# A decode kernel's last microseconds: the last head as single-column products for both chunks, the projections as one row, the output as four rows

## The chip, the cores and the metric

The kernel runs on one core of one Trainium2 chip. The metric is the device time of one execution in microseconds (us), lower is better. The profile was taken in one execution of each kernel; its span is 1.7 to 1.9 us shorter than the time of the same execution, so spans are compared with spans and times with times.

## The reference, cut to what matters

```python
# H, Sk, Dh = 32, 65536, 128;  D = 512;  F = 1792;  one token
g = sigmoid((x * gate_w).sum(-1))
q = (x @ wq).reshape(H, Dh)
p = softmax(q @ k_cache.T * Dh**-0.5)        # per head, over 65536 keys
a = concat(p @ v_cache) @ wo                 # 4096 -> 512
b = (silu(x @ w_gate) * (x @ w_up)) @ w_down
out = g * a + (1 - g) * b                    # 512 numbers
```

The two caches are 1.07 GB in bf16, and each byte is used once.

## The kernel before

The caches stream through three slots of 8 MB. A head is two chunks of 32768 keys, a partition holding 256 of them (`KPP`), so there are 64 chunks of keys and 64 of values; the last head is chunks 62 and 63. For a chunk, VectorE multiplies keys by the query, TensorE adds the products up by identity matmuls (`block`), VectorE sums the eight columns left over (`gather`), ScalarE takes the exponential. The values are then weighted in one of two forms. The wide form, used for chunks 0 to 62, has 64 matmuls with 4 columns of probabilities as weights and 512 columns of values moving; the wanted result is the diagonal, picked by four small products:

```python
def pv(n):
    ...
    mms(..., O_ps,
        [(P_sb[n % 2][:, g : g + VB], v[:, g : g + VB, :].rearrange("p a b -> p (a b)"))
         for g in range(0, KPP, VB)], ...)
    if c == last:
        act("O_sb", O_sb, O_ps, ACT.Copy, ["O_ps"], ["O_sb"])
        pending.append(h)          # diagonal() comes later
```

The column form has one matmul for each of the 256 keys of a partition, with a 128x128 tile of values as weights and one column moving. Before, it was used for chunk 63 only, piece by piece as the values land:

```python
V_END = [KPP // 2, KPP // 4, KPP // 8, KPP // 16, KPP // 16]      # 128, 64, 32, 16, 16
...
load("k", n, [EK] * (KPP // EK)); load("v", n, V_END)
turn_outputs(1)
rows("b_ps", wd, ..., hT, ...)                 # 4 x 14 one-column products into m_x
diagonal()
for i, j in enumerate(range(0, KPP, EK)):      # four blocks of the last keys
    block(n, j, EK)
    if i == 0:
        ...                                    # rest = (1 - g) * b
        rows("a_ps", wo, ..., M, ...)          # 4 x 32 one-column products
    if i == 2:
        ...                                    # rest += g * a   [128, 4]
    ...
for m in V_END:
    mms(("c", at), m_c[:, 0:1],
        [(v[:, j, :], P_sb[n % 2][:, j : j + 1]) for j in range(at, at + m)], ...)
    if at == 0:
        norm(h, H)
    at += m
dve("o_last", ... m_c[:, 0:1] * tot ...)                       # [128, 1]
rows("l_ps", wo_last, ..., o_last, "o_last", [0])              # 4 one-column products
dve("out_sb", ... m_x[:, :OT] * gval + rest ...)               # [128, 4]
dma("out", out[0, 0].rearrange("(p b) -> p b", b=OT), out_sb, ...)   # 128 pieces of 8 B
```

In chunk 62 the normalizer of the 31 heads before (`norm`: one matmul, a sum, a reciprocal; then `outputs`) is emitted right after the last block's sums, ahead of the gathers of the last two blocks; `turn_outputs(0)` follows behind them.

The softmax here doesn't subtract the row's maximum and nothing guards it: scores larger than these inputs give would overflow.

## Time and profile before

| | before |
|---|---|
| time, median of the 3 runs before the prediction | 2521.22 us (2519.79 to 2521.41) |
| span of the profiled execution | 2519.9 us |
| mean rate of the transfers over the span | 432 GB/s |
| last values landed | 2511.90 us |
| last column product ended | 2514.67 us |
| output issued / landed | 2515.62 / 2518.59 us |

The landings in this document are the completions that the trace records for each transfer; all times are counted from the start of the span.

From the page of the kernel before: the span, the transfers' busy share in 40 equal slices in tenths, and the bytes read with their rate.

```profile
span 2519.9 us, 15461 instructions
...
DMA  9999999999999999999999999999999999999998
...
HBM read 1087.77 MB, written 0.00 MB: 432 GB/s over the span
...
```

The stream of the caches is the kernel. In 39 of 40 slices the transfer engines are 90% busy or more.

The next lines are stretches of one microsecond at the end (start:end, length, then busy time and count of TensorE, weight loads, VectorE, ScalarE and GpSimd, then TensorE's granted clock as a share of full speed, the transfer engines' share and the rate in GB/s).

```profile
...
2510.00:2511.00 1.00, 1.00 (x44) 1.00 (x42) 0.29 (x2) 0.00 (x0) 0.00 (x0) 0.62 0.37 143
2511.00:2512.00 1.00, 0.44 (x17) 0.38 (x15) 0.00 (x0) 0.00 (x0) 0.00 (x0) 0.50 0.08 33
...
```

The stream runs dry between 2511 and 2512 us. What comes after is not covered by it.

From the timeline of the kernel before (start, duration, engine, line, operation, output and inputs, shapes, count; in brackets the idle time before and what ended it):

```profile
...
2463.50 0.42 DVE L478 TENSOR_REDUCE tot<-m_x 128x31 f32<-128x248 f32 x1 [4.14 <-PE m_x L251]
...
2464.51 0.68 DVE L363 TENSOR_REDUCE S_sb_81<-S_ps_101 128x64 f32<-128x512 f32 x1
...
2466.23 15.46 PE L251 MATMUL O_ps<-slot_65,P_sb_83 128*4 128x512 bf16 x64 [1.35 <-ACT P_sb_83 L288]
...
2477.82 4.42 DVE L338 TENSOR_TENSOR slot_67<-slot_67,q_bc_79 128x8192 bf16<-128x8192 bf16 x1 [12.02 <-DMA slot_67<-in_A_k_cache_dram]
...
2481.72 2.23 SPq L179 DMA_DIRECT2D slot_65<-in_A_v_cache_dram  x5
...
2484.76 0.39 PE L279 MATMUL S_ps_101<-slot_67,ident 128*128 128x512 bf16 x1
...
2488.22 4.38 PE L279 MATMUL m_x<-M,slot_66 128*128 128x1 bf16 x128
...
2492.68 5.08 PE L269 MATMUL S_ps_102<-slot_67,ident 128*128 128x512 bf16 x15
...
2498.41 4.42 DVE L338 TENSOR_TENSOR slot_67<-slot_67,q_bc_79 128x8192 bf16<-128x8192 bf16 x1
...
2506.35 3.35 PE L251 MATMUL m_c<-P_sb_84,slot_65 128*128 128x1 bf16 x128
...
2509.78 1.66 PE L251 MATMUL m_c<-P_sb_84,slot_65 128*128 128x1 bf16 x58
...
2512.66 2.01 PE L251 MATMUL m_c<-P_sb_84,slot_65 128*128 128x1 bf16 x70 [1.22 <-issue]
...
2515.07 0.27 PE L279 MATMUL m_x<-o_last,slot_66 128*128 128x1 bf16 x4 [0.41 <-DVE o_last L588]
2515.38 0.22 DVE L593 SCALAR_TENSOR_TENSOR out_sb<-m_x,gval,rest 128x4 bf16<-128x4 f32 x1 [0.45 <-PE m_x L279]
2515.62 0.35 SPq L179 DMA_DIRECT2D out_dram<-out_sb  x1
```

From top to bottom: the normalizer's sum at 2463.50, and the gather behind it; the wide products of chunk 62, until 2481.69; the last keys' first product, at 2477.82; the five loads of the last values, issued at 2481.72; the first sums of the last keys, waiting for TensorE until 2484.76; the 128 products with `wo`, between two sum groups; the next sums, in 5.08 us; the last vector product, late, at 2498.41; the columns of chunk 63, in three runs with a stop of 1.22 us in them; the four products and the last vector instruction of the closing chain; the store.

### The profile page before, as it was taken

The numbers are of one execution on the slowest core, as the hardware profiler recorded it, in microseconds if no ns is written. First come the engines' busy times: TensorE is split into PE (matmuls) and PEld (weight loads), VectorE is DVE, ScalarE is ACT, GpSimd is POOL, SyncE is SP. The second block draws the span as 40 slices with busy tenths as digits, with TensorE's granted clock in tenths as the row PEclk, the third lists the DMA queues.
The fourth block names the chain that finished last, engine by engine and source line by source line (L and its number), as shares of the span: only waits on it lengthen the run. The fifth ranks groups of instructions, "written<-read, shape, count | busy, mean of one in ns | idle before, by whom it ended". The sixth has DMA issues, their size and how long they took to land.

```text
span 2519.9 us, 15461 instructions
## 1 busy us (share of the span) xinstructions
PE 1980.9 (79%) x9115; PEld 410.4 (16%) x5153; DVE 1268.7 (50%) x290; ACT 97.9 (4%) x402; POOL 1.9 (0%) x9
## 2 busy tenths in 40 slices
PE   4787877877878778778787787787787877877888
PEld 1111111111111111111111111111111111111113
DVE  3455455464554554644645536446455455464454
ACT  0000000000000000000000000000000000000000
POOL 0000000000000000000000000000000000000000
PEclk8888988989889889899899899898988988989998
DMA  9999999999999999999999999999999999999998
GB/s 423 431 432 433 434 435 435 433 435 437 433 434 433 434 433 435 436 436 433 434 435 435 433 434 433 434 434 437 434 436 433 434 437 433 434 433 433 433 431 361
DMA packets 20903, 1088.04 MB, mean 432 GB/s; under 512 B 2450, under 2 KB 2580, under 8 KB 2836
## 3 DMA queue, kind: packets, MB, share of 16 engines
q1 hardware_dynamic: 20880, 1087.78, 99.7%
q8 instruction: 13, 0.21, 0.0%
q14 instruction: 6, 0.05, 0.0%
q10 hardware_dynamic: 4, 0.00, 0.0%
HBM read 1087.77 MB, written 0.00 MB: 432 GB/s over the span
## 4 chain that ended last, share of the span: by engine, by line
DMA 44%; PE 41%; DVE 13%; ACT 1%; issue 0%; another core or an unknown queue 0%; SPq 0%; DVEq 0%; ACTq 0%
PE O_ps L251 18%; DMA slot_67<-in_A_k_cache_dram 16%; DMA slot_65<-in_A_k_cache_dram 14%; DMA slot_66<-in_A_k_cache_dram 14%; PE S_ps_101 L269 11%; PE S_ps_102 L269 9%; DVE slot_67 L338 4%; DVE slot_66 L338 4%; DVE slot_65 L338 3%; DVE S_sb_82 L363 2%; PE m_c L251 1%; PE S_ps_101 L279 1%; PE m_x L279 1%; ACT P_sb_83 L288 1%; DMA slot_65<-in_A_wq_dram 0%; PE S_ps_102 L279 0%
## 5 line engine op out<-in xcount | busy, mean ns | idle before, releaser
L338 DVE TENSOR_TENSOR slot_67<-slot_67,q_bc_79 128x16384 bf16<-128x16384 bf16 (+1 forms) x28 | 208.2, 7469 | 143.8 <-DMA slot_67<-in_A_k_cache_dram 143.8
L363 DVE TENSOR_REDUCE S_sb_82<-S_ps_102 128x128 f32<-128x1024 f32 (+1 forms) x67 | 78.8, 1177 | 392.8 <-PE S_ps_102 L269 392.8
L338 DVE TENSOR_TENSOR slot_65<-slot_65,q_bc_78 128x16384 bf16<-128x16384 bf16 x22 | 190.2, 8689 | 146.9 <-DMA slot_65<-in_A_k_cache_dram 146.9
L338 DVE TENSOR_TENSOR slot_66<-slot_66,q_bc_78 128x16384 bf16<-128x16384 bf16 (+1 forms) x24 | 190.6, 7978 | 136.7 <-DMA slot_66<-in_A_k_cache_dram 121.2
L338 DVE TENSOR_TENSOR slot_66<-slot_66,q_bc_79 128x16384 bf16<-128x16384 bf16 x20 | 172.9, 8689 | 119.9 <-DMA slot_66<-in_A_k_cache_dram 119.9
L338 DVE TENSOR_TENSOR slot_65<-slot_65,q_bc_79 128x16384 bf16<-128x16384 bf16 x20 | 172.9, 8689 | 119.1 <-DMA slot_65<-in_A_k_cache_dram 119.1
L338 DVE TENSOR_TENSOR slot_67<-slot_67,q_bc_78 128x16384 bf16<-128x16384 bf16 x20 | 172.9, 8689 | 117.3 <-DMA slot_67<-in_A_k_cache_dram 117.3
L269 PE MATMUL S_ps_101<-slot_67,ident 128*128 128x512 bf16 x680 | 191.3, 450 | 0.0
L269 PE MATMUL S_ps_101<-slot_65,ident 128*128 128x512 bf16 x651 | 187.1, 458 | 0.0
L269 PE MATMUL S_ps_101<-slot_66,ident 128*128 128x512 bf16 x650 | 185.3, 455 | 0.0
L251 PE MATMUL O_ps<-slot_67,P_sb_83 128*4 128x512 bf16 x704 | 155.9, 383 | 27.9 <-ACT P_sb_83 L288 18.3
L251 PE MATMUL O_ps<-slot_65,P_sb_83 128*4 128x512 bf16 x704 | 155.2, 381 | 19.6 <-ACT P_sb_83 L288 19.6
L251 PE MATMUL O_ps<-slot_66,P_sb_84 128*4 128x512 bf16 x704 | 153.7, 379 | 19.3 <-ACT P_sb_84 L288 19.3
L251 PE MATMUL O_ps<-slot_65,P_sb_84 128*4 128x512 bf16 x640 | 139.7, 379 | 18.3 <-ACT P_sb_84 L288 18.3
L251 PE MATMUL O_ps<-slot_67,P_sb_84 128*4 128x512 bf16 x640 | 139.7, 379 | 18.3 <-ACT P_sb_84 L288 18.3
L251 PE MATMUL O_ps<-slot_66,P_sb_83 128*4 128x512 bf16 x640 | 139.7, 379 | 17.5 <-ACT P_sb_83 L288 17.5
L269 PE MATMUL S_ps_102<-slot_67,ident 128*128 128x512 bf16 x680 | 152.4, 382 | 0.0
L269 PE MATMUL S_ps_102<-slot_65,ident 128*128 128x512 bf16 x651 | 143.9, 379 | 0.0
L269 PE MATMUL S_ps_102<-slot_66,ident 128*128 128x512 bf16 x650 | 143.9, 379 | 0.0
L279 PE MATMUL S_ps_101<-slot_65,ident 128*128 128x512 bf16 x21 | 12.8, 608 | 134.5 <-DVE slot_65 L338 134.5
L279 PE MATMUL S_ps_101<-slot_66,ident 128*128 128x512 bf16 x22 | 13.1, 597 | 130.5 <-DVE slot_66 L338 130.5
L279 PE MATMUL S_ps_101<-slot_67,ident 128*128 128x512 bf16 x24 | 13.9, 580 | 125.4 <-DVE slot_67 L338 125.4
(89 smaller groups left out, 702.8 us busy)
## 6 DMA issues: line engine op xcount, KB each, us to landing
slot_66<-in_A_k_cache_dram SPq DMA_DIRECT2D x4, 2048.0 KB, 24.5
slot_67<-in_A_k_cache_dram SPq DMA_DIRECT2D x4, 2048.0 KB, 29.0
slot_65<-in_A_wq_dram SPq DMA_DIRECT2D x1, 4096.0 KB, 12.3
slot_66<-in_A_wo_dram SPq DMA_DIRECT2D x1, 4096.0 KB, 32.5
slot_65<-in_A_v_cache_dram SPq DMA_DIRECT2D x1, 4096.0 KB, 20.5
slot_65<-in_A_v_cache_dram SPq DMA_DIRECT2D x1, 2048.0 KB, 24.9
slot_65<-in_B_w_gate_dram SPq DMA_DIRECT2D x1, 1792.0 KB, 34.7
slot_65<-in_B_w_up_dram SPq DMA_DIRECT2D x1, 1792.0 KB, 38.4
```

The costliest lines, as they stand in the source:

```text
L251: ins = nc.tensor.matmul(out_ap, lhsT=a, rhs=b, start=start and i == 0, stop=stop and i == len(pairs) - 1,)
L269: ins = nc.tensor.add_instruction(mybir.InstMatmult(name=nc.get_next_instruction_name(), engine=mybir.EngineType.PE, ins=[nc.tensor.lower_ ...
L279: ins = nc.tensor.matmul(out_ap, lhsT=a, rhs=b, start=first, stop=last)
L288: "ACT", key, lambda: nc.scalar.activation(out=out_ap, in_=in_ap, func=func, **kw),
L338: "products", lambda: nc.vector.tensor_tensor(out=w, in0=w, in1=q_rep, op=ALU.mult),
L363: lambda: nc.vector.tensor_reduce(out=S_sb[b][:, :m], in_=S_ps[r][:, :m, :], axis=AXIS.X, op=ALU.add),
```

## The change

The intent is to let TensorE catch up before the last values land, and to store the output in longer pieces. Chunk 62 takes the column form, in three pieces, straight into the accumulation that chunk 63 continues, so the last head needs no diagonal. The projections with `w_down` and `wo` are turned round: one column of activations as weights, 512 columns moving, the result one row of 512 on one partition. Two evictions scale the rows, and eight products with a row of units lay them onto four partitions. The last head's product comes out on four partitions as well, and the output is stored as four rows of 256 B. The normalizer moves too: its matmul ahead of the third block of chunk 62, the rest of it behind the gathers. The diff, cut to its core:

```diff
@@ pv @@
-        last = CH - 2 if h == H - 1 else CH - 1          # (and every use of it)
@@ new @@
+    def column(n, pieces, at=0):
+        ...
+        for m in pieces:
+            mms(("c", n, at), m_c[:, 0:1],
+                [(v[:, j, :], P_sb[n % 2][:, j : j + 1]) for j in range(at, at + m)], ...,
+                start=(n == N - 2 and at == 0), stop=(n == N - 1 and at + m == KPP))
+            at += m
-    def rows(key, w_v, names, cols, cname, ks): ...      # one-column products
+    def row(key, w_v, names, cols, cname, ks, bank, bname):
+        mms(key, bank[0:1, :D], [(cols[:, k : k + 1], w_v[:, k, :]) for k in ks], ...)
@@ chunk 62 @@
+            if n == N - 2 and j == 2 * m:
+                sum_ps(0, H - 1)                         # first half of norm
             block(n, j, m)
-            elif n == N - 2 and j + m == KPP:
-                norm(0, H - 1)
-                outputs()
         ...
-            turn_outputs(0)
-        pv(n)
+            norm(0, H - 1)
+            outputs()
+        if n < N - 2:
+            pv(n)
+        else:
+            column(n, [KPP // 2, KPP // 4, KPP // 4])
@@ chunk 63 @@
+    turn_outputs(0)
     turn_outputs(1)
-    rows("b_ps", ...); diagonal()
+    row("b_ps", wd, ..., m_x, "m_x");  act("row_b", ... scale=ngval[0:1, :])
+    row("a_ps", wo, ..., m_sp, "m_sp"); act("row_a", ... scale=gval[0:1, :])
     for i, j in enumerate(range(0, KPP, EK)):
+        if i == 2:
+            mms("rest_ps", m_sp[:OT, :P],
+                [(unit[:, OT * q : OT * (q + 1)], r[:, P * q : P * (q + 1)])
+                 for r in (row_b, row_a) for q in range(OT)], ...)
+            act("rest4", rest4, m_sp[:OT, :P], ACT.Copy, ...)
         block(n, j, EK)
-        ...                                              # rest, a_ps, rest2
+    column(n, V_END[:1]); sum_ps(h, H); norm(h, H); column(n, V_END[1:], V_END[0])
-    o_last ... ; rows("l_ps", ...)
+    dve("Z", ... Z[:, :: OT + 1] = m_c[:, 0:1] * tot ...)
+    mms("l_ps", m_x[:OT, :P],
+        [(Z[:, OT * q : OT * (q + 1)], wo_last[:, 0, P * q : P * (q + 1)]) for q in range(OT)], ...)
-    dma("out", out[0, 0].rearrange("(p b) -> p b", b=OT), out_sb, ...)
+    dma("out", out[0, 0].rearrange("(i p) -> i p", p=P), out_sb, ...)
```

More of the change, by code (lines that the diff above doesn't have):

```diff
@@ L147 @@
     tot = sb("tot", [P, H], f32)
-    rest = sb("rest", [P, OT], f32)
+    rest4 = sb("rest4", [OT, P], f32)
+    row_b = sb("row_b", [1, D], f32)
+    unit = sb("unit", [1, OT * OT], f32)
+    Z = sb("Z", [P, OT * OT], bf16)
     o_row = sb("o_row", [H, Dh], bf16)
     M = sb("M", [P, H], bf16)
-    o_last = sb("o_last", [P, 1], bf16)
-    out_sb = sb("out_sb", [P, OT], bf16)
+    out_sb = sb("out_sb", [OT, P], bf16)
     S_ps = [psum.tile([P, HK, R], f32, name=f"S_ps{i}") for i in range(2)]
@@ L226 @@
     op("DVE", "oT0", lambda: nc.vector.memset(oT, 0.0), writes=["oT"])
+    op("DVE", "unit0", lambda: nc.vector.memset(unit, 0.0), writes=["unit"])
+    op("DVE", "unit1", lambda: nc.vector.memset(unit[:, :: OT + 1], 1.0), writes=["unit"])
+    op("DVE", "Z0", lambda: nc.vector.memset(Z, 0.0), writes=["Z"])
     op("DVE", "rowsum0", lambda: nc.vector.memset(rowsum, 0.0), writes=["rowsum"])
@@ L381, in pv @@
         s = where["v", n]
-        last = CH - 2 if h == H - 1 else CH - 1
         v = view(s, 0, KPP, Dh)
         mms(
-            ("pv", s, n % 2, c == 0, c == last), O_ps,
+            ("pv", s, n % 2, c == 0, c == CH - 1), O_ps,
             [
@@ L393, in pv @@
             [("P_sb", n % 2, u) for u in range(RS)] + units(s, 0, SLOT), ["O_ps"],
-            start=(c == 0), stop=(c == last),
+            start=(c == 0), stop=(c == CH - 1),
         )
-        if c == last:
+        if c == CH - 1:
             act("O_sb", O_sb, O_ps, ACT.Copy, ["O_ps"], ["O_sb"])
@@ L403, in diagonal @@
         mms(
-            ("diagonal", h == H - 1), m_c[:, 0:1],
+            "diagonal", m_c[:, 0:1],
             [(O_sb[:, j * Dh : (j + 1) * Dh], pick[:, j : j + 1]) for j in range(VB)],
-            ["O_sb", "pick"], ["m_c"], stop=(h < H - 1),
+            ["O_sb", "pick"], ["m_c"],
         )
-        if h < H - 1:
-            act("o_all", o_all[:, h : h + 1], m_c[:, 0:1], ACT.Copy, ["m_c"], [("o_all", h)])
+        act("o_all", o_all[:, h : h + 1], m_c[:, 0:1], ACT.Copy, ["m_c"], [("o_all", h)])
+    def column(n, pieces, at=0):
+        s = where["v", n]
+        v = view(s, 0, KPP, Dh)
+        for m in pieces:
+            mms(
+                ("c", n, at), m_c[:, 0:1],
+                [(v[:, j, :], P_sb[n % 2][:, j : j + 1]) for j in range(at, at + m)],
+                [("P_sb", n % 2, u) for u in range(at // EK, -(-(at + m) // EK))]
+                + units(s, at * Dh, (at + m) * Dh),
+                ["m_c"], start=(n == N - 2 and at == 0), stop=(n == N - 1 and at + m == KPP),
+            )
+            at += m
     def hidden():
@@ L456, in gate, with sum_ps @@
         )
-    def rows(key, w_v, names, cols, cname, ks):
-        group(
-            key,
-            [
-                (
-                    m_x[:, b : b + 1],
-                    [(w_v[:, k, bass.ds(b, P, OT)], cols[:, k : k + 1]) for k in ks],
-                )
-                for b in range(OT)
-            ],
-            names + [cname], ["m_x"],
-        )
-    def norm(h0, h1):
+    def row(key, w_v, names, cols, cname, ks, bank, bname):
+        mms(key, bank[0:1, :D], [(cols[:, k : k + 1], w_v[:, k, :]) for k in ks],
+            names + [cname], [bname])
+    def sum_ps(h0, h1):
         w = CH * RS
@@ L475, in norm @@
             ["ones", "rowsum"] + [("rowsum", i) for i in range(h0 * w, h1 * w)], ["m_x"])
+    def norm(h0, h1):
+        w = CH * RS
         dve(
@@ L553 @@
     load("v", n, V_END)
+    turn_outputs(0)
     turn_outputs(1)
-    rows("b_ps", wd, units(ws, 0, WO), hT, "hT", range(FT))
-    diagonal()
-    for i, j in enumerate(range(0, KPP, EK)):
-        block(n, j, EK)
-        if i == 0:
-            dve("rest", lambda: nc.vector.tensor_scalar_mul(rest, m_x[:, :OT], ngval),
-                ["m_x", "ngval"], ["rest"])
-            rows("a_ps", wo, units(ws, WO, WL), M, "M", range(H))
-        if i == 2:
-            dve(
-                "rest2",
-                lambda: nc.vector.scalar_tensor_tensor(
-                    out=rest, in0=m_x[:, :OT], scalar=gval, in1=rest, op0=ALU.mult, op1=ALU.add
-                ),
-                ["m_x", "gval", "rest"], ["rest"],
-            )
+    row("b_ps", wd, units(ws, 0, WO), hT, "hT", range(FT), m_x, "m_x")
+    act("row_b", row_b, m_x[0:1, :D], ACT.Copy, ["m_x", "ngval"], ["row_b"], scale=ngval[0:1, :])
+    row("a_ps", wo, units(ws, WO, WL), M, "M", range(H), m_sp, "m_sp")
+    row_a = O_sb[0:1, :D]
+    act("row_a", row_a, m_sp[0:1, :D], ACT.Copy, ["m_sp", "gval"], ["O_sb"], scale=gval[0:1, :])
+    for i, j in enumerate(range(0, KPP, EK)):
+        if i == 2:
+            mms(
+                "rest_ps", m_sp[:OT, :P],
+                [
+                    (unit[:, OT * q : OT * (q + 1)], r[:, P * q : P * (q + 1)])
+                    for r in (row_b, row_a)
+                    for q in range(OT)
+                ],
+                ["unit", "O_sb", "row_b"], ["m_sp"],
+            )
+            act("rest4", rest4, m_sp[:OT, :P], ACT.Copy, ["m_sp"], ["rest4"])
+        block(n, j, EK)
         while len(todo) > 1:
@@ L573 @@
     gather()
-    s = where["v", n]
-    v = view(s, 0, KPP, Dh)
-    at = 0
-    for m in V_END:
-        mms(
-            ("c", at), m_c[:, 0:1],
-            [(v[:, j, :], P_sb[n % 2][:, j : j + 1]) for j in range(at, at + m)],
-            [("P_sb", n % 2, u) for u in range(at // EK, -(-(at + m) // EK))]
-            + units(s, at * Dh, (at + m) * Dh),
-            ["m_c"], start=False, stop=(at + m == KPP),
-        )
-        if at == 0:
-            norm(h, H)
-        at += m
-    dve("o_last", lambda: nc.vector.tensor_scalar_mul(o_last, m_c[:, 0:1], tot[:, h:H]),
-        ["m_c", ("tot", h)], ["o_last"])
-    rows("l_ps", wo_last, units(ws, WL, WL + D), o_last, "o_last", [0])
+    column(n, V_END[:1])
+    sum_ps(h, H)
+    norm(h, H)
+    column(n, V_END[1:], V_END[0])
+    dve(
+        "Z",
+        lambda: nc.vector.tensor_scalar_mul(
+            Z[:, :: OT + 1], m_c[:, 0:1].to_broadcast([P, OT]), tot[:, h:H]
+        ),
+        ["m_c", ("tot", h)], ["Z"],
+    )
+    mms(
+        "l_ps", m_x[:OT, :P],
+        [(Z[:, OT * q : OT * (q + 1)], wo_last[:, 0, P * q : P * (q + 1)]) for q in range(OT)],
+        ["Z"] + units(ws, WL, WL + D), ["m_x"],
+    )
     dve(
@@ L593 @@
         lambda: nc.vector.scalar_tensor_tensor(
-            out=out_sb, in0=m_x[:, :OT], scalar=gval, in1=rest, op0=ALU.mult, op1=ALU.add
+            out=out_sb, in0=m_x[:OT, :P], scalar=gval[:OT, :], in1=rest4,
+            op0=ALU.mult, op1=ALU.add,
         ),
-        ["m_x", "gval", "rest"], ["out_sb"],
+        ["m_x", "gval", "rest4"], ["out_sb"],
     )
-    dma("out", out[0, 0].rearrange("(p b) -> p b", b=OT), out_sb, ["out"], ["out_sb"])
+    dma("out", out[0, 0].rearrange("(i p) -> i p", p=P), out_sb, ["out"], ["out_sb"])
     op("SP", "end", None, reads=["out"])
```

## The prediction

By "cold" it means a low granted clock: in the trace before, the first wide products of chunk 62 start 427 ns apart at a granted clock of 0.50, the later ones 216 ns apart at 1.00. The sum of three terms came to 2.9 us.

> **What bounds the kernel now.** The cache stream. The page shows the DMA engines at 9 tenths in 39 of 40 slices and 432 GB/s; 1088 MB at that rate is the 2520 us. Transfers land 24 to 36 us after issue (list of DMA issues), so more than a slot is always queued. The change does not touch the body; only what follows the last byte can move the time.
>
> **The end, before.** By the DMA share in short windows the stream stops between 2511 and 2512 us; the last two value pieces (issued about 2483.5, 28.0 us to landing) land about 2511.9. TensorE is late there. In the timeline the product of chunk 62 with the values is 64 matmuls of 512 columns, 2466.23 to 2481.69; the first sums of the last key chunk, whose data came at 2477.8, start only at 2484.75; the 128 one-column products of wo sit between two sum groups (2488.2 to 2492.6), the next sums run cold (5.08 us, not 3.40), and the last vector product starts at 2498.41. The last head's columns start at 2506.35, take 26 ns each (128 in 3.35 us) plus an unexplained 1.22 us stop ("issue" in the chain of waits), and end at 2514.68: 2.8 us after the last landing. o_last, four matmuls and out_sb take 0.94 us; output issued 2515.62, landing 3.0 us later; end 2519.9.
>
> **What changes.**
> - Chunk 62 as 256 columns: 256 x 26 ns = 6.7 us instead of 15.5; TensorE is free about 2473.5, not 2481.7. Its value slot is released up to 12 us sooner; the queue being full, this gains nothing.
> - Projections as rows: 14 + 32 matmuls of 512 columns at 218 ns (64 in 13.97 us), 10 us warm, perhaps 12 with a cold start, instead of 2.0 + 4.4. More work, but mostly while TensorE would wait for the last keys, and no longer between sum groups.
> - Added: eight single-row fp32 matmuls (estimate 2 to 3 us, from 0.58 us for two passes of 248 fp32 columns) and three evictions of about 0.6 us on the idle ScalarE. Off the path.
> - Columns then start about 2503 to 2504 and follow the landings, ending about 2512.4, 0.5 us after the last. Gain 2.3 us.
> - Closing chain: Z costs what o_last did; four 128-column matmuls instead of one-column ones, +0.2 us.
> - Output: four rows of 256 B instead of 128 descriptors of 8 B. [...] the trace has 3.0 for the present store. [...]
>
> Sum: 2.3 - 0.2 + 0.8 = 2.9 us, 0.1%. Predicted 2518.3 us, range 2516.5 to 2520.3. Faster by over 2%: 0.005; within 2%: 0.99; slower: 0.005.
>
> **What would show it.** Body unchanged, stream ending 2511 to 2512; columns of chunk 62 done in 6.5 to 8 us; first sums of the last keys at 2484 to 2487; last vector product near 2496; columns of chunk 63 begin before 2505 and their last piece waits for a DMA[...].
>
> **What would make it wrong.** Rows running cold (427 ns each, 20 us) and delaying the last sums, so that TensorE stays late; the 1.22 us stop falling in the last columns (gain about 1 us only); a store no quicker for its longer rows; a stream ending a microsecond later or sooner by chance.

## More of the kernel before

The wait of the transfer queue for its own store (engine, line, what it waited for, total, times, longest):

```profile
...
SPq L179 <- DMA out_dram<-out_sb: 2.6, 1, 2.6
...
```

## The result, and the profile after

The kernel after took 2518.39 us at the median of 4 runs (2518.15 to 2518.62), the kernel before, with one more run beside them, 2521.18 us (2519.79 to 2521.41). The ratio is 0.999, with a 95% interval from 0.9973 to 1.0007; a ratio here is the mean time of one kernel's runs over that of the other's of the same rounds, so not quite the ratio of the medians quoted. The difference is real all the same: in this whole study the kernel after ran 9 times, from 2518.15 to 2518.62 us, and the kernel before 31 times, from 2519.47 to 2522.82 us, and the two sets do not touch.

From the page of the kernel after, the same lines:

```profile
span 2516.7 us, 15579 instructions
...
DMA  9999999999999999999999999999999999999998
...
HBM read 1087.77 MB, written 0.00 MB: 432 GB/s over the span
...
```

The stream is unchanged. From the timeline of the kernel after:

```profile
...
2461.14 5.95 PE L257 MATMUL m_c<-P_sb_83,slot_65 128*128 128x1 bf16 x229
...
2464.52 7.07 SPq L181 DMA_DIRECT2D slot_65<-in_A_v_cache_dram  x5
2469.42 0.86 PE L257 MATMUL m_c<-P_sb_83,slot_65 128*128 128x1 bf16 x27 [2.33 <-issue]
...
2471.14 5.61 PE L257 MATMUL m_x<-slot_66,hT 128*1 128x512 bf16 x14
...
2476.59 7.07 PE L257 MATMUL m_sp<-slot_66,M 128*1 128x512 bf16 x32
...
2483.59 0.39 PE L285 MATMUL S_ps_103<-slot_67,ident 128*128 128x512 bf16 x1
...
2487.35 3.40 PE L275 MATMUL S_ps_104<-slot_67,ident 128*128 128x512 bf16 x15
...
2490.68 1.03 PE L257 MATMUL m_sp<-row_b,unit 1*4 1x128 f32 x8
...
2492.79 4.42 DVE L344 TENSOR_TENSOR slot_67<-slot_67,q_bc_79 128x8192 bf16<-128x8192 bf16 x1
...
2502.09 3.44 PE L257 MATMUL m_c<-P_sb_84,slot_65 128*128 128x1 bf16 x127 [1.20 <-ACT P_sb_84 L294]
...
2508.56 3.12 PE L257 MATMUL m_c<-P_sb_84,slot_65 128*128 128x1 bf16 x112
...
2512.12 0.77 PE L257 MATMUL m_c<-P_sb_84,slot_65 128*128 128x1 bf16 x16 [0.43 <-DMA slot_65<-in_A_v_cache_dram]
...
2513.20 0.59 PE L257 MATMUL m_x<-slot_66,Z 128*4 128x128 bf16 x4 [0.32 <-DVE Z L600]
2513.83 0.34 DVE L612 SCALAR_TENSOR_TENSOR out_sb<-m_x,gval,rest_96 4x128 bf16<-4x128 f32 x1 [0.68 <-PE m_x L257]
2514.20 0.34 SPq L181 DMA_DIRECT2D out_dram<-out_sb  x1
```

The columns of chunk 62 run from 2461.14 to 2470.28 with a stop of 2.33 us in them. The rows fill the time to 2483.66, and the first sums follow without a gap. The last vector product starts at 2492.79, 5.6 us sooner than before and 0.5 us after its keys landed (2492.31). The last 16 columns wait for a transfer.

From the chain of waits of the kernel after (start, duration, what):

```profile
...
2471.16 40.91 DMA slot_65<-in_A_v_cache_dram
...
```

The transfer queue's wait for its store in the kernel after:

```profile
...
SPq L181 <- DMA out_dram<-out_sb: 0.8, 1, 0.8
...
```

The queue waits 0.8 us for the store instead of 2.6. The chain now runs through the load of the last values: it landed at 2512.07 us. Before, the same landing was at 2511.90, and the chain at that time was TensorE's. The two spans differ by 3.2 us, and the traces split that as follows:

| stretch | before | after | difference |
|---|---|---|---|
| last landing | 2511.90 | 2512.07 | +0.17 |
| last landing to last column's end | 2.76 | 0.81 | -1.95 |
| last column's end to issue of the store | 0.96 | 1.31 | +0.35 |
| issue of the store to its landing | 2.97 | 1.18 | -1.79 |
| landing to end of span | 1.30 | 1.30 | 0 |

### The profile page after: what moved, and what is told of

The parts are those of the page before. It is cut to its first block, busy times and chain, and to the rows that moved or that the text cites. A ratio compares the mean times of both kernels' runs of the same rounds, so it can differ in the third digit from the quotient of the medians. Undisturbed runs are those within 1.5% of the kernel's fastest.

```text
span 2516.7 us, 15579 instructions
## 1 busy us (share of the span) xinstructions
PE 1972.7 (78%) x9177; PEld 410.3 (16%) x5215; DVE 1268.4 (50%) x291; ACT 99.2 (4%) x404; POOL 1.9 (0%) x9
## 4 chain that ended last, share of the span: by engine, by line
DMA 46%; PE 40%; DVE 13%; ACT 1%; issue 0%; another core or an unknown queue 0%; SPq 0%; DVEq 0%; ACTq 0%
PE O_ps L257 17%; DMA slot_67<-in_A_k_cache_dram 16%; DMA slot_65<-in_A_k_cache_dram 14%; DMA slot_66<-in_A_k_cache_dram 14%; PE S_ps_103 L275 11%; PE S_ps_104 L275 8%; DVE slot_66 L344 4%; DVE slot_67 L344 4%; DVE slot_65 L344 3%; DMA slot_65<-in_A_v_cache_dram 2%; DVE S_sb_82 L369 2%; PE m_c L257 1%; PE S_ps_103 L285 1%; ACT P_sb_83 L294 0%; DMA slot_65<-in_A_wq_dram 0%
## 5 line engine op out<-in xcount | busy, mean ns | idle before, releaser
L257 PE MATMUL O_ps<-slot_67,P_sb_83 128*4 128x512 bf16 x704 | 155.9, 383 | 28.1 <-ACT P_sb_83 L294 18.3
L257 PE MATMUL O_ps<-slot_66,P_sb_84 128*4 128x512 bf16 x704 | 153.7, 379 | 19.3 <-ACT P_sb_84 L294 19.3
L257 PE MATMUL O_ps<-slot_65,P_sb_83 128*4 128x512 bf16 x640 | 139.7, 379 | 18.3 <-ACT P_sb_83 L294 18.3
L257 PE MATMUL O_ps<-slot_67,P_sb_84 128*4 128x512 bf16 x640 | 139.7, 379 | 18.3 <-ACT P_sb_84 L294 18.3
L257 PE MATMUL O_ps<-slot_65,P_sb_84 128*4 128x512 bf16 x640 | 139.7, 379 | 18.3 <-ACT P_sb_84 L294 18.3
L257 PE MATMUL O_ps<-slot_66,P_sb_83 128*4 128x512 bf16 x640 | 139.8, 379 | 17.5 <-ACT P_sb_83 L294 17.5
```

What stands on the lines that cost most here:

```text
L257: ins = nc.tensor.matmul(out_ap, lhsT=a, rhs=b, start=start and i == 0, stop=stop and i == len(pairs) - 1,)
```

## The experiments

Twelve more runs were made: the kernel after once more, and eleven kernels built from one of the two with a part undone, done alone or changed. One table has what their traces show; the times are medians of 5 runs, except for the extra loads (one run). "Lag" is from the last landing to the end of the last column, "sums" the times in which the four sum groups of the last keys were issued, first start to last start of 16, and "stop" is a pause of over 1 us in the columns of chunk 63 that is not a wait for values, from one start to the next (a bracket in the timeline has the idle time alone, some 0.15 us less).

| kernel | time (range), us | columns end | lag | sums, us | stop after column, us | store, us |
|---|---|---|---|---|---|---|
| before (31 runs) | 2521.26 (2519.47 to 2522.82) | 2514.67 | 2.76 | 3.25, 4.92, 3.24, 3.25 | 186: 1.4 | 2.97 |
| normalizer moved alone | 2521.10 (2520.98 to 2521.56) | 2514.41 | 2.47 | 4.93, 5.62, 3.24, 3.25 | 186: 1.2 | 2.72 |
| chunk 62 as columns, normalizer moved | 2520.11 (2520.02 to 2521.47) | 2512.79 | 0.63 | 4.76, 4.92, 3.24, 3.25 | none | 2.79 |
| all but the columns of chunk 62 | 2519.97 (2519.27 to 2520.08) | 2513.77 | 1.95 | 3.25, 3.24, 3.25, 3.25 | 181: 1.9 | 1.17 |
| all, store in 8 B pieces | 2520.27 (2519.94 to 2520.49) | 2512.86 | 0.63 | 3.25 each | 127: 2.6 | 3.09 |
| four-row store alone | 2518.47 (2518.15 to 2520.39) | 2513.29 | 1.24 | 4.93, 4.77, 3.24, 3.25 | 184: 1.6 | 1.18 |
| store and normalizer | 2519.42 (2518.09 to 2519.99) | 2513.87 | 1.99 | 5.78, 4.57, 3.24, 3.25 | 184: 1.6 | 1.18 |
| columns, normalizer, store; no rows | 2518.41 (2518.37 to 2518.79) | 2513.09 | 0.66 | 6.13, 4.76, 3.24, 3.25 | none | 1.18 |
| after, again | 2518.32 (2518.19 to 2518.53) | 2513.03 | 0.95 | 3.25 each | 127: 2.7 | 1.18 |
| after, last piece halved | 2518.36 (2518.25 to 2518.40) | 2512.78 | 0.84 | 3.25 each | 127: 2.3 | 1.18 |
| after, 60 more weight loads | 2518.55 (one run) | 2513.05 | 0.63 | 3.25 each | none | 1.18 |
| after, both of these | 2518.03 (2517.93 to 2518.24) | 2512.74 | 0.42 | 3.25 each | none | 1.17 |

Times are those of all runs; the other columns are those of the one profiled execution, which is why a kernel with a wide range can have a lag that does not match its median. The row of the store alone is that of its mended run; its first run, told below, ended its columns at 2515.29, with a lag of 3.35 us and no stop.

### The kernel after, once more (after_again)

No edit: the yardstick beside the next three.

> The changed kernel once more, unaltered, as the yardstick on this chip. Every theory expects 2518.4 us, within 0.4, 2.8 us under the kernel before; output store landing 1.2 to 1.3 us after issue; a stop of TensorE of 2.3 to 2.6 us in the columns of chunk 62 and another in those of chunk 63, exactly 512 TensorE instructions apart.

Measured: 2518.32 us, 3.0 under the kernel before of the same rounds (2521.34), ratio 0.9989 (0.9975 to 1.0003). The store and the stop in chunk 63 (2.50 us) were as expected; the stop in chunk 62 was longer, 2.94 us. In the trace after, counting all instructions of TensorE and its sequencer from one stop (2467.1 us) to the next (2505.6 us) gives 512.

### Chunk 62 as columns and the normalizer moved, nothing else (cols_only)

From the kernel before: `column`, the split of `norm` and their places as in the change; projections and store untouched.

```diff
+            if n == N - 2 and j == 2 * m:
+                sum_ps(0, H - 1)
...
-        pv(n)
+        if n < N - 2:
+            pv(n)
+        else:
+            column(n, [KPP // 2, KPP // 4, KPP // 4])
...
-    diagonal()
```

> The kernel before with only chunk 62 as columns; projections stay columns (wo still between two sum groups) and the store stays 128 pieces of 8 B. Parts that add up would give the 1.8 us by which the columns end earlier in the trace after: 2519.4 us. My theory is that they do not add: without the rows TensorE idles from about 2473 to 2482 and goes cold, so the first sums of the last keys start at 2482.2 instead of 2484.75 but take 4.5 to 6 us instead of 3.8, the wo products follow, and the last vector product starts at 2497 to 2498.5: gain only 0 to 1.5 us, 2519.7 to 2521.2. Store landing 2.9 to 3.1 us after issue in either case.

Measured: 2520.11 us, 1.2 under the kernel before, four of five runs within 0.2 us of it and one at 2521.47. The time lies in the range of the theory. From its timeline:

```profile
...
2482.60 0.61 PE L279 MATMUL S_ps<-slot,ident 128*128 128x512 bf16 x1 [10.65 <-DVE slot L338]
...
2483.00 4.73 PE L269 MATMUL S_ps<-slot,ident 128*128 128x512 bf16 x15
...
2492.04 5.08 PE L269 MATMUL S_ps<-slot,ident 128*128 128x512 bf16 x15
...
2497.77 4.42 DVE L338 TENSOR_TENSOR slot<-slot,q_bc 128x8192 bf16<-128x8192 bf16 x1
...
```

The first sums start at 2482.60, after 10.65 us of an idle TensorE, and they and the next group run slow (4.76 and 4.92 us against 3.25), as the theory has it; the last vector product starts at 2497.77, hardly sooner than the 2498.41 before. In this execution the columns still end 0.63 us after the last landing, 1.9 us sooner than before: they began 0.65 us sooner, and they met no stop of TensorE, where those of the kernel before lost 1.22 us.

### Rows and four-row store, chunk 62 in the wide form (rows_only)

```diff
-        if n < N - 2:
-            pv(n)
-        else:
-            column(n, [KPP // 2, KPP // 4, KPP // 4])
+        pv(n)                       # with the diagonal of before
...
+    diagonal()                      # after turn_outputs(1)
```

> The changed kernel with chunk 62 as 64 wide products and a diagonal again; rows and four-row store kept. If the parts add, the store's 1.8 us less 0.4 for the closing chain remain: about 2519.8 us. My theory: the 10 us of rows now start after 2481.7 and push the first sums of the last keys to about 2492, the columns end at 2516.5 to 2519, and the time is 2522 to 2524.5, slower than the kernel before, although the store still lands 1.2 to 1.4 us after issue.

Measured: 2519.97 us, 1.4 under the kernel before and 1.65 over the kernel after. My theory failed. The wide products began at 2461.85, not 2466.2, and took 13.97 us, so the first sums started at 2487.8 instead of 2492, and the columns ended at 2513.77. I had left the moved normalizer out of the account. Without the columns of chunk 62 the lag is 1.95 us, with them 0.81. But that does not show that the columns are needed beside the rows, for this kernel's columns of chunk 63 met a late stop:

```profile
...
2508.40 1.50 PE L257 MATMUL m_c<-P_sb,slot 128*128 128x1 bf16 x53
...
2511.61 2.16 PE L257 MATMUL m_c<-P_sb,slot 128*128 128x1 bf16 x75 [1.71 <-issue]
...
```

They began at 2504.97 us; without the 1.71 us they could have ended at 2512.06, only 0.24 us after the last landing, so they would have waited for it. What the stops are is asked below, under `more_loads`.

### The store in 128 pieces of 8 B (store_8b)

Wrong order of the output.

```diff
-    dma("out", out[0, 0].rearrange("(i p) -> i p", p=P), out_sb, ["out"], ["out_sb"])
+    dma("out", out[0, 0].rearrange("(q i b) -> i q b", i=OT, b=OT),
+        out_sb.rearrange("i (q b) -> i q b", b=OT), ["out"], ["out_sb"])
```

> The changed kernel with its four rows written in 128 pieces of 8 B (wrong order of the output on purpose). If the number of small pieces makes the old store slow, landing is 2 to 4 us after issue [...] and the time 2519.2 to 2521. If it is the number of partitions and engines taking part, landing stays at 1.2 to 1.5 us and the time at 2518.4 to 2518.7. All else as in the changed kernel.

Measured: 2520.27 us, 1.95 over the kernel after of the same rounds. All else was the same, and the queue waited for the store:

```profile
...
SPq L181 <- DMA out_dram<-out_sb: 2.8, 1, 2.8
...
```

Against 0.8 us. From issue to landing it took 3.09 us, on four partitions, about as long as the store of before took on 128 (2.97). So it is the cutting into 128 pieces of 8 B that makes the old store slow, not the number of partitions. Number and size of the pieces changed together, and no run separates them. The traces also show where the time goes: the last packet of the store is done 1.04 us after issue before, 1.24 us in this run and 0.85 us in the kernel after, and the landing follows 1.92, 1.86 and 0.32 us later. So most of the difference, 1.6 us of 1.8 against the kernel before and 1.5 of 1.9 against this run, is a wait after the pieces have moved. The pieces to a completion do not set it either: the store of before has 16 completions in the trace and this one 4, so 8 pieces to each in one and 32 in the other.

### The normalizer moved, alone (norm_only)

```diff
+            if n == N - 2 and j == 2 * m:
+                sum_ps(0, H - 1)
             block(n, j, m)
...
-            elif n == N - 2 and j + m == KPP:
-                norm(0, H - 1)
-                outputs()
...
-            turn_outputs(0)
+            norm(0, H - 1)
+            outputs()
         pv(n)
...
+    turn_outputs(0)                 # chunk 63, ahead of turn_outputs(1)
```

> The kernel before with one thing moved: the normalizer of the first 31 heads (its matmul, its sum, its reciprocal, the scaling of the outputs, the turn) no longer stands ahead of the last two gathers of chunk 62. Everything else is as before: 64 wide products, columns for the projections, 128 pieces of 8 B. If this move is what freed TensorE early (in the run with rows alone the wide products started at 2461.9 instead of 2466.2), the wide products run from 2461.9 to 2475.9 and the time is that of the run with chunk 62 as columns alone, 2520.1 within 0.5. If the column form of chunk 62 is what counts, the time stays at 2521.0 to 2521.5.

Measured: 2521.10 us, 0.3 under the kernel before of the same rounds and within the spread of its runs, and 1.0 over the kernel with the columns as well. My theory failed again: the move alone is worth nothing that these runs can show. The wide products started at 2464.20, 2.0 us sooner than before, in 13.97 us; the first sums started at 2482.24, 2.5 us sooner, but they and the next group ran slow (4.93 and 5.62 us against 3.25 for a group at a granted clock of 1.00), and the columns began at 2506.23 against 2506.35. What the move gave, the slow sums took, and the stop after column 186 stayed where it was.

### The four-row store alone (store_only, then store_right)

From the kernel before; the rest, 128 by 4, is turned by one fp32 product with an identity, and `Z`, `l_ps`, `out_sb` and the store are those of the change.

```diff
+        if i == 3:
+            mms("rest_ps", m_sp[:OT, :P], [(rest, ident_f)], ["rest", "ident_f"], ["m_sp"])
+            act("rest4", rest4, m_sp[:OT, :P], ACT.Copy, ["m_sp"], ["rest4"])
         block(n, j, EK)
```

> The kernel before with only the four-row store: the rest is turned from 128 by 4 to 4 by 128 with one fp32 product with an identity, the last head's product comes out as four rows. TensorE's schedule stays as before, so the columns still end near 2514.7. If the store's gain stands alone (1.8 us in landing, less 0.4 in the closing chain): 2519.8 to 2520.3, store landing 1.1 to 1.3 us after issue. If the store only helps after an early end, no gain: 2521 to 2521.5.

The output came out wrong, because the old weight tiles take every fourth column and the new rows are blocks of 128. The store and the closing chain are the intended ones, so its times are told: 2518.62 us, with runs at 2518.14, 2518.22, 2518.62, 2520.32 and 2520.78. Mended, with the tiles in blocks,

```diff
-                    [(w_v[:, k, bass.ds(b, P, OT)], cols[:, k : k + 1]) for k in ks],
+                    [(w_v[:, k, b * P : (b + 1) * P], cols[:, k : k + 1]) for k in ks],
```

it was run again:

> The four-row store alone on the kernel before, as the earlier run of it, now with the output in the right order (the weight tiles taken in blocks of 128 columns). Its gain at an equal end of the columns is 1.8 us in landing less 0.4 in the closing chain: 1.4 us, so 2519.9 at the median. The earlier run had 2518.1 to 2518.6 three times and 2520.3 and 2520.8 twice. If TensorE is still the last to finish and its clock varies from run to run, the runs again spread over 1.5 us or more, and the time never falls under 2518.1. If the store were worth 2.8 us by itself, the runs would lie within 0.5 us of 2518.5.

Measured, and correct: 2518.47 us, runs at 2518.15, 2518.28, 2518.47, 2518.87 and 2520.39. The store lands 1.18 us after issue in both. The median gain, 2.8 us, is twice what I expected. The two kernels are not quite one, though. Taking the tiles in blocks instead of every fourth column, the only edit between them, shortened the 128 products with `wo` from 4.40 to 3.37 us and the 56 with `w_down` from 2.03 to 1.55 (median start to start 33 and 25 ns). So this kernel, and the next two, which have blocks as well, contain a second change. The mean is 2519.22 us with the old tiles and 2518.83 with blocks, against 2521.11 for the 31 runs of before: gains of 1.9 and 2.3 us, of which the store and the closing chain explain 1.4. The rest must lie in when the columns end. That varies from run to run: the ten runs of the two kernels spread over 2.6 us, and the two profiled executions end their columns at 2515.29 and 2513.29. Why these kernels more often end them early is left open; the spread of the kernel before, 3.3 us, is too wide to settle it.

### Store and normalizer, without columns or rows (norm_store)

The two diffs above together, with the tiles in blocks.

> Moved normalizer and four-row store, with chunk 62 as 64 wide products and the projections as columns. If the column form of chunk 62 is needed for the full gain: 2521.1 less 1.4, about 2519.7, within 0.5. If store and normalizer suffice: 2518.2 to 2518.6.

Measured: 2519.42 us, with runs from 2518.09 to 2519.99. That is 1.0 us over the kernel with the column form of chunk 62 (2518.41); in two of five runs there was no difference. The profiled execution again met a late stop, of 1.42 us after column 184; without it its columns could have ended at 2512.45, 0.57 us after the last landing, so this run does not show that the column form is needed either.

### Columns, normalizer and store, without the rows (cols_store)

The kernel with chunk 62 as columns, with the store's diff and the tiles in blocks.

> Chunk 62 as columns, moved normalizer and four-row store, but the projections as columns (no rows, no single-row products; the rest turned by one fp32 product). If the rows only serve to make the four-row form and one turning product serves as well: 2520.1 less 1.4, about 2518.7, within 0.3 of the changed kernel. If the rows matter because they keep TensorE warm and wo out from between the sum groups: 2519.3 or more.

Measured: 2518.41 us, within 0.1 us of the kernel after, runs from 2518.37 to 2518.79. So the projections as rows, their 46 wide products and the eight single-row products, buy nothing but the four-row form, and one turning product gives that as well (here beside one-column products that the tiles in blocks had made 1.0 us shorter). The two kernels that store in 8 B pieces say the same: 2520.27 us with the rows, 2520.11 without (and with the old tiles). The sums of this kernel ran slow (6.13 and 4.76 us in the first two groups), and the end was still set by the last landing, 0.66 us before the last column's end.

### The last piece halved (finer_end)

```diff
-    V_END = [KPP // 2, KPP // 4, KPP // 8, KPP // 16, KPP // 16]
+    V_END = [KPP // 2, KPP // 4, KPP // 8, KPP // 16, KPP // 32, KPP // 32]
```

> The changed kernel with the last value piece cut in two (8 and 8 instead of 16). If the stream's last landing bounds the end, only 8 columns instead of 16 follow it: 0.2 to 0.4 us less than the changed kernel, 2518.0 to 2518.2, first byte to last unchanged. If TensorE bounds the end, or the smaller pieces slow the stream, the time is 2518.3 or more.

Measured: 2518.36 us, no gain. The trace shows why: after the last landing only 8 columns are left, but TensorE pauses 0.4 us after column 253, where no wait for values stands. That is exactly 256 instructions of TensorE after its stop behind column 127; the next run asks what happens there.

### Sixty more weight loads in the last sums (more_loads)

```diff
-                    if a is held:
+                    if hold and a is held:
...
-            names + ["ident"], [("S_ps", r)],
+            names + ["ident"], [("S_ps", r)], hold=(n < N - 1),
```

> The changed kernel with a weight load of its own for each of the 64 sum products of the last key chunk, 60 TensorE instructions more, hidden behind products of 218 ns. If the stops are waits for a block of 256 instructions, the stop in the columns of chunk 62 stays after column 229 and the one in chunk 63 moves from after column 127 to after column 97 (30 pairs earlier), still 512 instructions after the first, each with one instruction transfer just before its end. If the stop is a wait for data or for the probabilities, it stays after column 127. Time 2518.2 to 2518.8 either way, since the columns still wait for the last landing.

This run asks what the stops are. They are not waits for data: in the kernel after the stop after column 127 stands within a piece of 128 that had landed at 2501.96 as a whole. The list of transfers in the stretch of that stop (2505.6 to 2506.7 us) has one transfer of instructions:

```profile
...
q8 instruction: 1, 0.02, 5.5%
...
```

Such a transfer is 16384 bytes, and this one took 0.96 us; the stop ends 2.4 us after its start at 2505.66. In chunk 62 the transfer starts at 2467.12 and the stop ends at 2469.42. Between the stops stand 512 instructions, with one transfer more among them, at 2475.26, that made no stop. Counted back from the end of the stop in chunk 63, the three stretches of 256 instructions before it begin at 2463.7, 2469.4 and 2502.0 us, and each has one such transfer, at 2467.1, 2475.3 and 2505.7. In the kernel before, counted back from its stop in the same way, they begin at 2482.9, 2491.1 and 2507.9, with transfers at 2485.6, 2494.3 and 2510.3. So each of these six stretches has one transfer of 16384 bytes; the fourth stretch back has none in either trace. That a stop is a wait for such a transfer is my reading.

With 60 more instructions my expectation, a stop moved to column 97, was not met: there is no such stop left. Lines of its timeline:

```profile
...
2502.44 3.35 PE L257 MATMUL m_c<-P_sb,slot 128*128 128x1 bf16 x128 [0.70 <-DMA slot<-in_A_v_cache_dram]
...
2507.20 1.87 PE L257 MATMUL m_c<-P_sb,slot 128*128 128x1 bf16 x64 [1.19 <-DMA slot<-in_A_v_cache_dram]
2510.01 1.01 PE L257 MATMUL m_c<-P_sb,slot 128*128 128x1 bf16 x32 [0.94 <-DMA slot<-in_A_v_cache_dram]
...
2512.46 0.59 PE L257 MATMUL m_c<-P_sb,slot 128*128 128x1 bf16 x16 [0.63 <-DMA slot<-in_A_v_cache_dram]
...
```

All pauses now stand at the edges of the pieces and wait for a transfer. The transfers of instructions were at 2493.02, 2507.82 and 2511.16 us. Counted on from the earlier stop, the stretch of 256 that ends at column 97 now begins while TensorE is still at the sums of the last keys and lasts 11.4 us (2493.51 to 2504.87); 256 instructions of single-column products last 256 x 13 ns = 3.3 us (13 ns is half of the 26 ns for a load and its product). In the nine executions with a stop in chunk 63 (1.2 to 2.7 us from start to start), the stretch that ends at the stop began 4.7 to 6.1 us before the stop's end, and its transfer started 2.3 to 3.7 us after that beginning; in this run a transfer started 0.5 us before it. That the longer stretch is why the stop is gone is my reading. What sets off a transfer no trace here shows. Shown are the spacing by multiples of 256, and the transfer of instructions before the end of each stop: in all nine the next column starts 1.2 to 1.5 us after that transfer ended (2506.63 and 2508.09 in the kernel after, 2511.24 and 2512.66 in the kernel before). Where a kernel has no such stop, it came to its next multiple of 256 at least 1.6 us after the transfer before it had ended. And 60 instructions more did away with the stop. The pause after column 253 in `finer_end` is of the same kind: its transfer ended at 2511.33, and the next column started at 2512.54. The time, 2518.55 us in one run of unknown state, is no better than that of the kernel after: there the stop lies before the last landing and costs nothing. In the kernel before, whose TensorE was late, the stop after column 186 stood in the chain of waits.

### The halved piece and the loads together (finer_loads)

Both diffs.

> The changed kernel with the last value piece cut into 8 and 8 and the 60 extra hidden weight loads. In the run with the finer end alone a stop of 0.4 us after column 253 ate the gain, and the extra loads remove that stop. If that is right, the columns end within 0.6 us of the last landing and the time is 0.2 to 0.3 us under the changed kernel: 2518.0 to 2518.2. If the extra instruction transfer delays the last landing by as much, 2518.3 to 2518.6.

Measured: 2518.03 us, runs from 2517.93 to 2518.24, output correct. The columns end 0.42 us after the last landing, though that landing itself was a little later (2512.33). From its timeline:

```profile
...
2511.13 0.98 PE L257 MATMUL m_c<-P_sb,slot 128*128 128x1 bf16 x24 [0.22 <-DMA slot<-in_A_v_cache_dram]
2512.37 0.37 PE L257 MATMUL m_c<-P_sb,slot 128*128 128x1 bf16 x8 [0.25 <-DMA slot<-in_A_v_cache_dram]
...
```

This is the fastest kernel, by 0.3 us against the medians of the kernel after (2518.32 and 2518.39), though the ranges overlap by 0.1 us. They were not run side by side; the kernel before had medians of 2521.26 us in these rounds and of 2521.34 and 2521.18 in the other two sets.

## Why the prediction was right

The time was predicted as 2518.3 us and is 2518.39. It is right for the reason given, that only what follows the last byte can move the time, but the terms of its sum were off; that they made up for one another is luck.

- **The stream bounds the kernel, and the change does not touch it.** Right: 432 GB/s in both, the last landing at 2511.90 and 2512.07 us. The early release of the value slot (the first load issued at 2464.52 instead of 2481.72) gained nothing, as foreseen.
- **TensorE catches up and the columns follow the landings.** Right in kind: first sums at 2483.6 (foreseen 2484 to 2487), last vector product at 2492.8 (foreseen near 2496, so better), columns from 2502.1 (foreseen before 2505), the last piece waiting for a transfer. The size, 2.3 us, measured 1.8: the columns end 0.81 us after the landing, not 0.5. Not all of it is TensorE catching up. In the kernel before, the stop of 1.22 us ended at 2512.66, after the last landing; without it the columns could have ended at 2513.45, 1.55 us after the landing instead of 2.76. In the kernel after, the stop falls at column 127, long before the last landing, and costs nothing. How much of the gain is the earlier start and how much the moved stop is open: the kernel before with a few weight loads more, which would tell, was not run. The prediction named a stop in the last columns as a risk; that it fell elsewhere was luck.
- **The columns of chunk 62 in 6.5 to 8 us.** Wrong by the stop: 9.1 us, of which 2.3 is the stop. The 26 ns for a pair held (229 pairs in 5.95 us).
- **What frees TensorE.** Incomplete: I put all of it down to the column form and did not read the moved normalizer in the diff. Moved alone it gave 0.3 us, within the spread; with the columns 1.2 us. The columns without the move were not run, and in the three kernels that lack only the columns (`norm_only`, `rows_only`, `norm_store`) a late stop of 1.1 to 1.7 us stands where their gain would be read, so the column form is not shown to be needed.
- **The rows, "no longer between sum groups".** Of no worth by themselves: without them (but with tiles in blocks), and with `wo` still between the groups, the time is 2518.41 us. In the kernel after they took 12.5 us, from 2471.14 to 2483.66, close to the "perhaps 12 with a cold start".
- **The closing chain, +0.2 us.** It measured +0.35, mostly as the four products took 0.59 us instead of 0.27, and `out_sb` 0.34 instead of 0.22.
- **The store, -0.8 us.** Undersized by more than half: 1.79 in the traces, and 1.95 in the times, by the run that undoes it alone. The 0.8 us was my estimate, which no trace showed: the trace before has only its own store, 3.0 us. The new store landed 1.17 to 1.18 us after issue in every kernel that stores four rows.

So the store was given too little and TensorE's lateness too much: 2.3 - 0.2 + 0.8 = 2.9 foreseen, 1.8 - 0.35 + 1.8 = 3.2 between the two profiled executions. By the times, undoing the store's form alone takes back 1.95 of the 3.0 us, and 1.1 us remain for TensorE's part and the place of its stop.

There is one more effect I did not foresee. The kernel before runs anywhere from 2519.47 to 2522.82 us, the kernel after from 2518.15 to 2518.62. In the kernels with one-column projections the second sum group, and mostly the first, took 4.6 to 6.1 us instead of 3.25. The granted clock goes with it: in the fourteen profiled executions the 43 groups at 1.00 took 3.24 to 3.25 us, and the 13 at 0.55 to 0.72 took 4.57 to 6.13. In the stretch from 2492.4 to 2497.8 us, which holds such a group, the granted clock of the kernel before was 0.68; in the kernel after it was 1.00 in both of its first groups. The stretches of the kernel before and, below, of the kernel after (columns as above; the clock is the third number from the end):

```profile
...
2492.40:2497.80 5.40, 5.40 (x24) 0.24 (x6) 1.18 (x2) 0.00 (x0) 0.00 (x0) 0.68 0.97 416
...
```

and of the kernel after:

```profile
...
2483.60:2487.20 3.60, 3.60 (x18) 0.16 (x2) 3.46 (x1) 0.68 (x1) 0.00 (x0) 1.00 1.01 432
2487.10:2490.80 3.70, 3.70 (x19) 0.19 (x4) 3.55 (x2) 0.35 (x2) 0.00 (x0) 1.00 1.11 478
...
```

Where TensorE finishes last, such variation lands in the time; where the last landing does, it is hidden. The kernel without rows shows that: slow sums, yet its five runs lie within 0.42 us. That this is the whole cause of the spread before is argued, not shown: only one execution of each kernel was profiled. In the kernel after it is the rows that get the low clock: behind the columns of chunk 62 the 14 products with `w_down` start 426 ns apart (median), at a granted clock of 0.54 from 2471.2 to 2476.5 us, while in `rows_only`, where wide products stand ahead of them, they start 216 ns apart.

## What to carry to other kernels

In a kernel bound by a stream, read the end as a sum from the last landing: the lag of the consumer, the closing chain, the store. Look at the pieces of the final store, for a kilobyte in 128 pieces of 8 B cost 1.8 us more than in four rows of 256 B, more than any rearrangement of matmuls gave by itself. And when a long run of very short instructions sits at the end, look for pauses that wait for nothing, spaced by a fixed number of instructions (512, in one run 256, here); 60 more instructions earlier on, hidden behind long ones, took such a pause away here. The pauses also fell elsewhere from one kernel to the next (after column 127, 181, 184 or 186, or nowhere), so check where they fall before you credit an edit with the rest of the gain.
